# Turned rows in two tiles, and seven weight pieces split ahead of the last routing

## The chip, the core and the metric

The kernel runs on one core of a Trainium2 chip. What is measured is the device time of one execution, in microseconds (us), as the median of several runs. Engines are named as in the profile: PE is TensorE's matmuls and PEld its weight loads, DVE is VectorE, ACT is ScalarE, POOL is GpSimd, and SP is the engine that issues most DMAs. "SPq" marks what SP's sequencer does, the issuing of a DMA above all.

## The reference

Three layers run one after the other: an attention with capped scores, a dense gated MoE layer, and a sparse MoE with one expert for each token.

```python
# attention: B=4, H=12, S=448, D=64
scores = cap * tanh(q @ k.T / sqrt(D) / cap)
x = softmax(scores) @ v                       # then rows of 768 for 1792 tokens
# first MoE: 768 -> 1536 -> 768
x = (silu(x @ w_gate) * (x @ w_val)) @ w_out
# second MoE: 8 experts, 768 -> 1024 -> 768
do = x @ w_skip > 0                           # other tokens keep x
e = argmax(x[do] @ w_route); g = softmax(...)[e]
out[do] = x[do] + g * (relu(x[do] @ w1[e]) @ w2[e])
```

Products whose accuracy matters are made of three: each operand is split into a high and a low part (float32r), and high x high, high x low and low x high are added up in PSUM (`mm3`, `mm3_`).

## The kernel before

All instructions stand in an order that is written out by hand; on each engine they run in that order, and semaphores hold an instruction until what it reads is there.

The tokens come in four batch rows of 448. Attention works on pairs of heads, six pairs for a row. The first MoE of a row has 36 units: 24 of `g` and `v` (gate and value columns) and 12 of `y` (output columns, each in two halves). Unit `w` of 144 does 18 products of 128x448. `OPENING` is the order of the first row's attention; then `FIRST_UNITS` is the order inside each of the first 36 units and `UNITS` that of the others. While the units of row `b` run, the attention of row `b + 1` runs between them. In the first 36 units the weights also arrive as 64 bit numbers and are converted on DVE (`convert`), kept in DRAM (`keep_w`, tensor `ws`), and read again from there for the rows that follow (`load_w`, tile `raw64` of pool `r64`, four buffers). `round_w` (ACT) and `rest_w` (DVE) split a unit's weights two units ahead. "piece" in the unit orders is `load_w`, "loads" brings the heads of a later pair, "keep" is `keep_w`.

When an output column group is done (`rows_end`), `turn_rows` multiplies it with the routing weights on PE and turns it on DVE into the tile `row`, two units after; one unit later `store_rows` sends it to the output with four DMAs from SP ("store" in the orders). There is one buffer of `row`, and in the last batch row a second one, `so["row"]`, for odd groups. In `FIRST_UNITS` "store" is the last word, behind "piece", "keep" and "loads".

The second MoE works on slots: up to 128 tokens of one expert. An expert's weights come as eight pieces of 128x1536 (four of `w1`, four of `w2`). A piece is loaded by SP into a raw room (`so["raw"]`, `load_next`) and split into a pair of rooms (`so["pair"]`, `split_next`): ACT makes the high part, DVE the low part. `first(0)` to `first(3)` and `second(0)` to `second(3)` each use one piece; `piece()` hands it out, and once `so["auto"]` is set it splits ahead until `AHEAD` pieces are ready. Slot 0 holds tokens of the first three rows only. It is routed while the last row's units run; its expert's and slot 1's expert's weights are fetched early (`FETCHED`). `SPLITS` names the units, counted from the end, behind which one piece is split and another loaded. The last row's attention rooms serve as three raw rooms and three pairs (`open_early`), and two pairs more come from the first MoE's input (`more`).

After the last unit the left side's rooms are given back and `open_late` opens others: seven raw rooms, one pair, and tiles for the gathered rows. `LATE` is the order of what follows: the routing of the last row on DVE (`choose`, `ranks`, `gates`, `tiles`, `places`, `at`, `entries`, `listed`, `experts`) and, beside it, slot 0 on PE (`first1` to `second3`; `hidden0` and `hidden1` turn the hidden rows, `lows0` and `lows1` make their low parts; `split` splits one piece; `rows1` turns the input rows of slot 1). `gates` has an exponential on ACT, `count` two products on PE. When the list is there, POOL gathers the rows of slots 1 to 7 (`gather`). Slots 1 to 7 then run through `slot`.

At the very start `big` is loaded into a register of every engine: it chooses between two versions of the whole kernel, and the branch on it stands behind the first transposes.

Of the kernel before, what the change touches and what calls it, by code (L numbers as in the profile page):

```python
# [7 lines left out]
F32 = mybir.dt.float32  # L8
F32R = mybir.dt.float32r
# [17 lines left out]

LENGTHS = (5, 6, 5, 6, 5, 5)

AHEAD = 4  # L30

SPLITS = (11, 10, 9, 7, 6)


STEPS = {0: 6, 1: 2, 2: 3, 3: 3, 4: 3, 5: 4, None: 4}
# [16 lines left out]
""".split()  # L52
FIRST_UNITS = """
    out weigh sum scores1 roundw bits gate hidden after after after bits loww dn products both bits tanh1 exp1
    tanh2 exp2 turn abs bits split last bits scores2 bits piece keep loads logits count rows chain turnl store
""".split()
UNITS = """
    out turnl weigh sum scores1 scores2 products fold count logits rows hidden split loads tanh1 exp1 add1 turn
# [1 line left out]
    chain store  # L60
""".split()
LATE = """
    choose first1 count first2 hidden0 gates ranks tiles places lows0 at entries first3 split second0 listed hidden1
    gather experts lows1 second1 split second2 split rows1 second3 gather gather gather gather gather gather
""".split()


# [1 line left out]
def tile_attn_moe_moe(  # L69
# [15 lines left out]
    nc = tc.nc  # L85
    B, H, S, D = q.shape
# [9 lines left out]
    PIECE = 1536  # L96
# [12 lines left out]
    big_i = const.tile([128, 1], I32, name="big_i")  # L109
# [15 lines left out]
    count = const.tile([T, E], F32, name="count")  # L125
# [9 lines left out]
    rows = const.tile([T, 128], mybir.dt.bfloat16, name="rows")  # L135
# [245 lines left out]
    def whole(exact):  # L381
        with ExitStack() as ph:

            def pools(side):
                stack = ph.enter_context(ExitStack())

                def pool(name, bufs, **kw):
                    kw.setdefault("reuse_waits", "tile")
                    return stack.enter_context(tc.tile_pool(name=name, bufs=bufs, side=side, **kw))

                return stack, pool

            _, pool = pools("left")
            keep_p = pool("keep", 1)
            left, pool = pools("left")
            one_p = pool("one", 1)
            r64_p = pool("r64", 4)
            w_p = pool("w", 3)
            y_p = pool("y", 2)
            ps_v = pool("ps_v", 1, space=PSUM)  # L400
# [1 line left out]
            right, pool = pools("right")  # L402
# [208 lines left out]
            W_END = B * NU  # L611
# [72 lines left out]
            cur, terms = {}, {}  # L684
# [61 lines left out]
            def turn_rows(b, j):  # L746
                x2 = cur.pop(("x2", j))
                cur["lp", j] = lp = ps_m.tile([128, T], F32, name="mo")
                for c in range(NC):
                    nc.tensor.matmul(  # L750
                        lp[32 * c:32 * c + 32], lhsT=w9[:, j], rhs=x2[:, T * c:T * c + T], start=True, stop=True
                    )

                cur["row", j] = row = so["row"] if b == B - 1 and j % 2 else one_p.tile([128, S], F32, name="row")
                nc.vector.transpose(out=row, in_=x2)

            def store_rows(b, j):
# [58 lines left out]
            chain = [None, None]  # L816
# [13 lines left out]
            so = {"raw": [], "pair": [], "xg": [], "auto": False}  # L830
# [18 lines left out]
            def open_late():  # L849
                left.close()  # L850
                _, pool = pools("left")
                p = pool("late", 1)
                psum = pool("ps_l", 1, space=PSUM)
                so["xg"] += [p.tile([128, DM], F32, name=f"xg{i}") for i in range(1, NSTATIC)]
                so["raw"] += [p.tile([128, PIECE], F32, name=f"raw{i}") for i in range(7)]
                so["pair"] += [[p.tile([128, PIECE], F32R, name=f"{n}4") for n in ("gh", "gl")]]
                so["late"] = p.tile([T, 1600], F32, name="late_room")
                so["hid"] = p.tile([128, F2], F32, name="hid")
                so["o"] = [p.tile([128, DM], F32, name=f"o{i}") for i in range(3)]
                so["last"] = psum.tile([128, 512], F32, name="last")  # L860
                so["py"] = psum.tile([128, 2, 512], F32, name="py")
                for xg in so["xg"][1:]:
                    nc.gpsimd.memset(xg, 0.0)
# [27 lines left out]
            def turn_x(s):  # L891
                xh, xl = so["x"]
                for kk in range(0, KD, 3):
                    turned(xh[:, kk:kk + 3], xl[:, kk:kk + 3], so["xg"][s % NSTATIC][:, 128 * kk:128 * kk + 384])
# [100 lines left out]
            at = {load_part: 8}  # L995
# [158 lines left out]
            for w in range(W_END):  # L1154
                if w == W_END - NU:
                    open_early()
                unit(w)
                if w == W_END - NU + 2 * KF:

                    more = keep_p.tile([128, 2 * KD * S], F32R, tag="xhl", name="more")  # L1160
                    so["pair"] += [[more[:, 0:PIECE], more[:, PIECE:2 * PIECE]], [more[:, 2 * PIECE:3 * PIECE], so["odd"]]]
                    while load_next():
                        pass
                if w == W_END - 6:
                    while chain[0] is not None:
                        step("v", 1)
                        step("p", 1)
                    turn_x(0)
                if W_END - w in SPLITS:
                    split_next()  # L1170
                    load_next()
# [69 lines left out]
    with tc.manual_schedule():  # L1241
        nc.sync.dma_start(out=cap_sb, in_=cap.to_broadcast([128, 1]))
        for i, (queue, src) in enumerate(((nc.sync, q), (nc.scalar, k))):
            for j in range(2):
                queue.dma_start(out=first_pair()[:, i, :, j], in_=src[0, j].rearrange("(c p) d -> p c d", c=NC))
        for i in range(8):
            load_block(1, i)
        nc.gpsimd.memset(ident, 1.0)
        nc.gpsimd.affine_select(
            out=ident, in_=ident, pattern=[[1, 128]], compare_op=ALU.is_equal, fill=0.0, base=0,  # L1250
            channel_multiplier=-1,
        )
        nc.vector.memset(ones, 1.0)
        nc.scalar.activation(out=old, in_=ones[0:T, 0:1], func=ACTF.Tanh)
        nc.vector.tensor_reduce(
            alike[:, 0], ident.rearrange("p (a b) -> p b a", b=32), axis=AX.X, op=ALU.add
        )
        nc.vector.tensor_copy(alike[:, 1], alike[:, 0])
        nc.vector.memset(w9, 0.0)
        nc.vector.tensor_scalar(big_i, cap_sb, cap_sb, CAP_FAST * CAP_FAST, op0=ALU.mult, op1=ALU.is_gt)  # L1260
        nc.vector.tensor_scalar(inv_sb, cap_sb, float(D) ** 0.5, None, op0=ALU.mult)
        nc.vector.reciprocal(inv_sb, inv_sb)

        with tc.tile_pool(name="setup", bufs=5) as setup:

            def count_off(dst, **kw):
                ti = setup.tile(list(dst.shape), I32, name="ti")
                nc.gpsimd.iota(ti[:], **kw)
                nc.vector.tensor_copy(dst, ti)

            count_off(rank8, pattern=[[-1, E]], base=E, channel_multiplier=0)
            count_off(rows, pattern=[[1, 128]], base=1, channel_multiplier=0)
            count_off(steps, pattern=[[128, JM]], base=0, channel_multiplier=0)
            count_off(slots, pattern=[[1, MAXSLOT]], base=0, channel_multiplier=0)
            nc.vector.tensor_scalar(number, rank8, -1.0, float(E), op0=ALU.mult, op1=ALU.add)
            nc.vector.tensor_tensor(
                before, rank8.unsqueeze(1).to_broadcast([T, E, E]), rank8.unsqueeze(2).to_broadcast([T, E, E]),
                op=ALU.is_gt,
            )

            count_off(tok, pattern=[[T, NT]], base=-65536, channel_multiplier=1)
            nc.gpsimd.memset(oh, 0.0)
            nc.gpsimd.memset(above, 0.0)
            nc.gpsimd.affine_select(
                out=lt, in_=ones[0:T], pattern=[[1, T]], compare_op=ALU.is_ge, fill=0.0, base=0,
                channel_multiplier=-1,
            )

        with tc.tile_pool(name="first", bufs=2, space=PSUM) as first_p:
            for i in range(2):  # L1290
                ps = first_p.tile([128, S], F32, name="turned")
                for c in range(NC):
                    nc.tensor.transpose(
                        ps[:, T * c:T * c + T], first_pair()[:, i, c].rearrange("p h d -> p (h d)"), ident[0:T, 0:T]
                    )
                (nc.scalar.copy if i else nc.vector.tensor_copy)(first_turned()[:, i], ps)
        big = nc.values_load(big_i[0:1, 0:1], min_val=0, max_val=1)
        with tc.If(big > 0) as cmp:
            whole(True)
        with cmp.Else():  # L1300
            whole(False)
# [31 lines left out]
```

## Time and profile before

| | us |
|---|---|
| median of 3 runs | 926.13 |
| lowest and highest run | 925.58, 926.15 |
| the profiled execution | 925.63 |
| its span, first to last instruction | 923.8 |
| PE busy | 893.8 (97%) |
| DVE busy | 628.3 (68%) |
| ACT busy | 506.7 (55%) |
| POOL busy | 109.3 (12%) |

[...] Times in the rows below are microseconds from the start of the span. A row of the timeline gives the start, the duration (of all together where several instructions are merged), the engine, the line of the kernel, the operation with what it writes and reads, and in brackets how long the engine stood idle before it and what ended that. PE's matmuls overlap, so their durations are longer than the distance from one to the next.

### The profile page before, as it was taken

To read this page: it belongs to the slowest core of one execution; us is meant where nothing else is said; L and a number is where in the kernel's file an instruction comes from. 1 tells how busy PE (TensorE), PEld (TensorE's weight loads), DVE (VectorE), ACT (ScalarE), POOL (GpSimd) and SP (SyncE) were. 2 spreads that over 40 slices of the span, in tenths; PEclk is the share of its full clock that TensorE was granted. 3 is DMA by queue.
4 is the path that set the end of the run, shared out by engine and by line. 5 is a ranking of instruction groups with operands and counts; after the bars stand their busy time and mean duration, and the time that the engine had idled before them with its cause. 6 is when DMAs were issued, how large, how long until landed. Compare 5 with 4: busy or idle time off the path is not lost.

```text
span 923.8 us, 12689 instructions
## 1 busy us (share of the span) xinstructions
PE 893.8 (97%) x4700; PEld 696.2 (75%) x4700; DVE 628.3 (68%) x920; ACT 506.7 (55%) x587; POOL 109.3 (12%) x72
## 2 busy tenths in 40 slices
PE   5999999999799999999999999999999998899996
PEld 2336776677477877787778877889999887789996
DVE  2768999998637656654657656535765636999994
ACT  4995675657245455535546456223333423877782
POOL 1000000000002221222122230200000013110001
PEclk9999999999899999999999999999999998999999
DMA  6997889888676444524673322254262738999970
GB/s 120 185 241 205 229 235 252 235 243 230 161 151 166 107 97 100 132 53 96 142 168 113 85 78 91 66 133 147 69 240 73 236 72 313 360 381 348 382 251 7
DMA packets 226336, 161.50 MB, mean 175 GB/s; under 512 B 159180, under 2 KB 186828, under 8 KB 226256
## 3 DMA queue, kind: packets, MB, share of 16 engines
q1 hardware_dynamic: 224048, 157.12, 60.0%
q0 software_dynamic: 1280, 3.16, 1.0%
q8 instruction: 41, 0.67, 0.3%
q14 instruction: 39, 0.32, 0.1%
q10 hardware_dynamic: 928, 0.23, 0.1%
HBM read 140.80 MB, written 22.81 MB: 177 GB/s over the span
## 4 chain that ended last, share of the span: by engine, by line
PE 86%; DVE 5%; ACT 4%; DMA 2%; issue 2%; SPq 1%; POOL 0%; POOLq 0%; DVEq 0%; ACTq 0%
PE mo L680 19%; PE mo L682 17%; PE mo L681 17%; PE ps L458 7%; PE bank L513 6%; PE py L937 3%; PE py L936 3%; PE py L935 2%; PE ph L936 2%; PE ph L935 2%; PE ph L937 2%; PE tp L884 1%; PE mo L547 1%; ACT arena L467 1%; ACT arena L474 1%
## 5 line engine op out<-in xcount | busy, mean ns | idle before, releaser
L680 PE MATMUL mo<-xhl,wh 128*128 128x448 f32 x576 | 215.0, 373 | 0.0
L682 PE MATMUL mo<-xhl,wl 128*128 128x448 f32 x576 | 210.4, 365 | 0.0
L681 PE MATMUL mo<-xhl,wh 128*128 128x448 f32 x576 | 210.3, 365 | 0.0
L355 DVE TENSOR_TENSOR wl<-raw,wh 128x768 fp32r<-128x768 f32 x108 | 115.7, 1071 | 71.4 <-ACT wh L667 69.8
L667 ACT CAST wh<-raw 128x768 fp32r<-128x768 f32 x108 | 89.7, 831 | 87.9 <-PE mo L681 61.2
L680 PEld LDWEIGHTS mo<-xhl,wh 128*128 128x128 f32 x576 | 108.1, 188 | 27.3 <-issue 8.1
L682 PEld LDWEIGHTS mo<-xhl,wl 128*128 128x128 f32 x576 | 108.2, 188 | 8.9 <-DVE wl L355 0.2
L681 PEld LDWEIGHTS mo<-xhl,wh 128*128 128x128 f32 x576 | 108.3, 188 | 7.9
L680 PE MATMUL mo<-hh,wh 128*128 128x448 f32 x288 | 108.5, 377 | 0.3 <-ACT x L727 0.3
L682 PE MATMUL mo<-hh,wl 128*128 128x448 f32 x288 | 105.5, 366 | 0.0
L681 PE MATMUL mo<-hl,wh 128*128 128x448 f32 x288 | 105.5, 366 | 0.0
L719 ACT ACTIVATE s<-mo 128x448 f32<-128x448 f32 x48 | 26.0, 541 | 114.5 <-PE mo L682 111.6
L458 PE MATMUL ps<-qkt 64*112 64x448 f32 x368 | 82.6, 568 | 0.0
L467 ACT ACTIVATE arena<-ps,inv_sb 112x896 f32<-112x896 f32 x72 | 68.6, 1004 | 5.6 <-PE ps L458 5.5
L502 POOL TENSOR_TENSOR sums<-arena 112x896 f32<-112x896 f32 x11 | 23.3, 2114 | 394.5 <-ACT arena L474 394.5
L474 ACT ACTIVATE arena<-arena,cap_sb 112x1792 f32<-112x1792 f32 x36 | 64.5, 1792 | 1.1
L680 PEld LDWEIGHTS mo<-hh,wh 128*128 128x128 f32 x288 | 54.3, 189 | 13.3 <-issue 8.7
L722 DVE SCALAR_TENSOR_TENSOR s<-s,mo 128x448 f32<-128x448 f32 x48 | 29.6, 617 | 42.6 <-PE mo L682 42.3
L682 PEld LDWEIGHTS mo<-hh,wl 128*128 128x128 f32 x288 | 54.2, 188 | 4.6
L681 PEld LDWEIGHTS mo<-hl,wh 128*128 128x128 f32 x288 | 54.4, 189 | 4.1
L513 PE MATMUL bank<-arena,arena 112*64 112x448 f32 x264 | 54.9, 548 | 1.6 <-ACT w L638 0.8
L458 PEld LDWEIGHTS ps<-qkt 64*112 64x112 f32 x368 | 29.6, 175 | 34.9 <-issue 29.3
(257 smaller groups left out, 1430.1 us busy)
## 6 DMA issues: line engine op xcount, KB each, us to landing
raw<-ws SPq DMA_DIRECT2D x54, 768.0 KB, 4.8
raw<-in_moe_w_dram SPq DMA_DIRECT2D x41, 768.0 KB, 6.6
ws<-w SPq DMA_DIRECT2D x36, 384.0 KB, 5.9
pair_room<-in_moe_w_dram SPq DMA_DIRECT2D x16, 768.0 KB, 6.6
raw<-in_moe_w_gate_dram SPq DMA_DIRECT2D x12, 768.0 KB, 5.3
raw<-in_moe_w_val_dram SPq DMA_DIRECT2D x12, 768.0 KB, 5.8
raw<-in_moe_w_out_dram SPq DMA_DIRECT2D x12, 768.0 KB, 5.2
arena<-in_v_dram SPq DMA_DIRECT2D x24, 224.0 KB, 5.1
```

The source lines that it names most:

```text
L355: engine.tensor_tensor(low, full, high.bitcast(F32), op=ALU.subtract)
L458: nc.tensor.matmul(ps[:, i, 0:S], lhsT=qkt[rows_, 1, T * c:T * c + T], rhs=qkt[rows_, 0], start=True, stop=True)
L467: nc.scalar.activation(out=t[:, j], in_=ps[:, :, 0:S], func=ACTF.Tanh, scale=inv_sb[0:T])
L474: nc.scalar.activation(out=ts[part], in_=ts[part], func=ACTF.Exp, scale=cap_sb[0:T])
L513: nc.tensor.matmul(pv[64 * i:64 * i + 64], lhsT=hd["vn"][:, i, c], rhs=hd["t"][c // 2][:, c % 2, i], start=c == 0, stop=c == NC - 1,)
L667: nc.scalar.copy(wh, w32s[w])
L680: nc.tensor.matmul(ps, lhsT=wh, rhs=mh, start=start, stop=False)
L681: nc.tensor.matmul(ps, lhsT=wh, rhs=ml, start=False, stop=False)
L682: nc.tensor.matmul(ps, lhsT=wl, rhs=mh, start=False, stop=stop)
L935: nc.tensor.matmul(ps, lhsT=sh, rhs=wh, start=start, stop=False)
L936: nc.tensor.matmul(ps, lhsT=sh, rhs=wl, start=False, stop=False)
L937: nc.tensor.matmul(ps, lhsT=sl, rhs=wh, start=False, stop=stop)
```

## The change

- `FIRST_UNITS`: "store" moves from the end of a unit to a place ahead of "piece".
- `row` gets two buffers.
- Pool `r64` moves to the part of the left side that stays open to the end, so its four rooms outlive the first MoE. Ahead of the splits behind the last two units, two pairs are made of these four rooms. `SPLITS` gets the entries 2 and 1: two more pieces are split behind units 142 and 143, and two more loaded.
- `open_late` opens five raw rooms instead of seven and no pair. So there are eight raw rooms in all instead of ten, and seven pairs instead of six.
- `AHEAD` is 5 instead of 4.
- `LATE`: "ranks" and then "gates" come right behind "count", before "first2" and "hidden0" (before: "gates" then "ranks" behind "hidden0"). The last "split" stands behind "rows1" instead of ahead of it.
- The register load of `big` stands ahead of the first transposes.

```diff
-AHEAD = 4
-
-SPLITS = (11, 10, 9, 7, 6)
+AHEAD = 5
+
+LATER = 5
+SPLITS = (11, 10, 9, 7, 6, 2, 1)
 FIRST_UNITS = """
     out weigh sum scores1 roundw bits gate hidden after after after bits loww dn products both bits tanh1 exp1
-    tanh2 exp2 turn abs bits split last bits scores2 bits piece keep loads logits count rows chain turnl store
+    tanh2 exp2 turn abs bits split last bits scores2 bits store piece keep loads logits count rows chain turnl
 LATE = """
-    choose first1 count first2 hidden0 gates ranks tiles places lows0 at entries first3 split second0 listed hidden1
-    gather experts lows1 second1 split second2 split rows1 second3 gather gather gather gather gather gather
+    choose first1 count ranks gates first2 hidden0 tiles places lows0 at entries first3 split second0 listed hidden1
+    gather experts lows1 second1 split second2 rows1 split second3 gather gather gather gather gather gather
             keep_p = pool("keep", 1)
+            r64_p = pool("r64", 4)
             left, pool = pools("left")
             one_p = pool("one", 1)
-            r64_p = pool("r64", 4)
-                cur["row", j] = row = so["row"] if b == B - 1 and j % 2 else one_p.tile([128, S], F32, name="row")
+                cur["row", j] = row = so["row"] if b == B - 1 and j % 2 else one_p.tile([128, S], F32, name="row", bufs=2)
-                so["raw"] += [p.tile([128, PIECE], F32, name=f"raw{i}") for i in range(7)]
-                so["pair"] += [[p.tile([128, PIECE], F32R, name=f"{n}4") for n in ("gh", "gl")]]
+                so["raw"] += [p.tile([128, PIECE], F32, name=f"raw{i}") for i in range(LATER)]
+                if W_END - w in (1, 2):
+
+                    so["pair"] += [[r64_p.tile([128, PIECE], F32R, tag="raw64", name=n) for n in ("gh", "gl")]]
                 if W_END - w in SPLITS:
                     split_next()
                     load_next()
+        big = nc.values_load(big_i[0:1, 0:1], min_val=0, max_val=1)
         with tc.tile_pool(name="first", bufs=2, space=PSUM) as first_p:
...
-        big = nc.values_load(big_i[0:1, 0:1], min_val=0, max_val=1)
         with tc.If(big > 0) as cmp:
```

## Rows read from the trace of the kernel before

**Rows 1.** The page: busy time of PE, and one group of DMA issues.

```profile
PE 893.8 (97%) x4700; PEld 696.2 (75%) x4700; DVE 628.3 (68%) x920; ACT 506.7 (55%) x587; POOL 109.3 (12%) x72
...
raw<-in_moe_w_dram SPq DMA_DIRECT2D x41, 768.0 KB, 6.6
```

**Rows 2.** The timeline of DVE where the first row's units turn output rows.

```profile
228.76 0.27 DVE L768 COPY lgt<-mo 128x112 f32<-128x112 f32 x1
239.24 0.65 DVE L755 STREAM_TRANSPOSE row<-x 128x448 f32<-128x448 f32 x1 [10.21 <-DMA out_dram<-row]
...
245.68 0.64 DVE L572 STREAM_TRANSPOSE dn<-mo 128x448 f32<-128x448 f32 x1
```

**Rows 3.** The timeline of SP in the same stretch.

```profile
228.91 0.39 SPq L619 DMA_DIRECT2D raw<-ws  x1
...
232.76 4.77 SPq L761 DMA_DIRECT2D out_dram<-row  x4
```

**Rows 4.** The timeline of PE in the same stretch.

```profile
236.25 0.94 PE L547 MATMUL mo<-head_room,ones 112*32 112x448 f32 x8
...
246.38 0.39 PE L578 MATMUL bank<-dn,alike 64*64 64x14 f32 x4 [5.28 <-DVE dn L572]
```

**Rows 5.** Stretches of 1 us: length, busy us by engine, granted clock, DMA share, GB/s.

```profile
245.00:246.00 1.00, 0.00 (x0) 0.00 (x0) 1.00 (x2) 1.00 (x2) 0.00 (x0) 0.61 1.01 267
252.00:253.00 1.00, 1.00 (x6) 0.92 (x6) 0.96 (x2) 0.00 (x0) 0.00 (x0) 0.98 1.02 409
...
774.00:775.00 1.00, 1.00 (x6) 1.00 (x5) 0.97 (x4) 0.00 (x0) 0.00 (x0) 0.64 1.01 393
...
781.00:782.00 1.00, 1.00 (x5) 0.70 (x5) 1.00 (x2) 0.11 (x1) 1.00 (x1) 0.95 0.53 128
```

**Rows 6.** The timeline of DVE in the last routing and slot 1.

```profile
768.39 0.19 DVE L212 TENSOR_REDUCE gate<-late_room 112x4 f32<-112x32 f32 x1 [3.71 <-ACT late_room L211]
...
772.12 0.68 DVE L355 TENSOR_TENSOR rl<-tp,rh 128x512 fp32r<-128x512 f32 x1
...
774.49 1.75 DVE L355 TENSOR_TENSOR gl<-head_room,gh 128x1536 fp32r<-128x1536 f32 x1
776.89 0.20 DVE L1191 TENSOR_TENSOR lists<-lists,last 128x42 f32<-128x42 f32 x1 [0.64 <-PE last L256]
...
778.92 0.67 DVE L355 TENSOR_TENSOR rl<-tp,rh 128x512 fp32r<-128x512 f32 x1
...
784.66 1.02 DVE L355 TENSOR_TENSOR xgl<-tp,xgh 128x384 fp32r<-128x384 f32 x2 [1.46 <-ACT xgh L885]
786.59 1.02 DVE L969 SCALAR_TENSOR_TENSOR o<-py,lists,xg 128x768 f32<-128x768 f32 x1 [0.91 <-PE py L937]
...
797.53 0.69 DVE L355 TENSOR_TENSOR rl<-tp,rh 128x512 fp32r<-128x512 f32 x1
```

**Rows 7.** The timeline of PE in the last routing and slot 1.

```profile
764.63 0.39 PE L195 MATMUL last<-above,ones 112*112 112x40 f32 x2 [0.18 <-DVE above L188]
...
772.86 0.44 PE L937 MATMUL py<-more,rl 128*128 128x384 f32 x1 [2.82 <-DVE rl L355]
...
783.62 0.60 PE L884 MATMUL tp<-ident,xg 128*128 128x128 f32 x4
...
789.33 0.50 PE L936 MATMUL ph<-gl,xgh 128*128 128x512 f32 x1 [2.40 <-DVE gl L355]
...
797.95 0.34 PE L935 MATMUL py<-gh,rh 128*128 128x384 f32 x1
```

**Rows 8.** POOL's first gather in the timeline, and the landing of all eight gathers.

```profile
778.10 1.01 POOL L870 DMA_INDIRECT xg<-out_dram,idx  x1 [14.64 <-DVE late_room L231]
...
DMA to landing us min/median/max: 3.8/6.7/8.0
```

**Rows 9.** The timeline of DVE behind the last unit's products.

```profile
758.96 0.27 DVE L770 TENSOR_TENSOR lgt<-lgt,mo 128x112 f32<-128x112 f32 x1 [6.97 <-PE mo L750]
```

**Rows 10.** The timeline of ACT in the opening.

```profile
19.49 0.92 ACT L638 ACTIVATE w<-raw 128x768 f32<-128x768 f32 x1 [0.34 <-DMA raw<-in_moe_w_gate_dram]
```

## The prediction

> **What bounds the kernel now.** I read the page first: TensorE (PE) is busy for 97% of the span [rows 1], so a change pays only where PE waits or runs at its lower clock, or if it gives PE less to do. This change leaves PE's work as it is. So I went through the busy time of 10 to 100 us stretches and looked for those in which PE is not full. Four are left: the opening, a hole near 245 us, two holes between 770 and 790 us, and the end after the last product. Everywhere else PE is at 100%, so what a stage saves stays saved: behind each hole PE alone sets the pace.
>
> The hole near 245 us: PE waits 5.28 us for a transposition on VectorE (DVE) [rows 4]. DVE is late because it stood idle for 10.21 us before it could write the second turned row [rows 2]: the single row tile was still being stored. SP issued that store at 232.76 us, although DVE had turned the row before it went on to the work at 228.76 us: SP first stood before a piece load that it got out at 228.91 us, and then issued keeps and loads [rows 3]. The granted clock shows what follows: it falls at about 245.4 us and is back at 252 us [rows 5].
>
> The holes of the last routing: PE waits 2.82 us for the low half of the turned hidden rows, then 2.40 us for the first split of slot 1 [rows 7]. After the first the clock is at its lower level from about 774.3 to 781.1 us [rows 5]; after the second it doesn't fall.
>
> **The change part by part.**
>
> **Two row tiles, and the store ahead of the piece load.** The second row goes to its own tile, so DVE's idle 10.21 us ends [rows 2] (two later and far shorter waits of this kind lie beside full PE and are worth nothing). Next late: the transposition that PE waited for needs the sum products, which start at 236.25 us and take 0.94 us [rows 4]; DVE does it by 237.8 us, and PE wants it at 246.38 - 5.28 = 241.1 us. So the wait goes whole, with 3.3 us to spare. The clock's fall goes with it: from 246.38 to 252.0 us PE worked 5.6 us at half its speed, of which half, 2.8 us, comes back; I take 2.6, since not every instruction there doubled. Sum: 5.3 + 2.6 = **7.9 us**. On SP the four stores now stand in front of the piece load, the keep and the pair loads. If they take as long as before, 4.77 us [rows 3], the piece load moves from 228.91 to at most 232 us; it is fetched five units ahead, some 20 us before its use, so this costs nothing. What else is queued behind it, a pair load, is used at the end of the pair's next round, also over 8 us later. If that cover were gone, it would cost 3 us.
>
> **Two more splits before the routing.** Each is a copy on ScalarE (ACT) and a subtraction on DVE, 1.75 us as at 774.49 [rows 6]. They are placed where DVE stands idle for 6.97 us [rows 9] and ACT at least as long, and two splits need 3.5 us: nothing is pushed. Their rooms are those of the first MoE's weights, whose last reader on DVE has ended by then. DVE now turns one row after the first split instead of before it, and SP stores it some 3 us later, but still ahead of the last row's store. Cost 0; without the cover 3.5 us.
>
> **Gates after the ranks, their exponential issued first.** DVE waits 3.71 us for that exponential [rows 6], since ACT had the turned hidden rows ahead of it. Now ranks can begin when the count is there, at 764.63 + 0.39 us [rows 7], and the exponential is done meanwhile. The whole DVE chain moves up by 3.3 us. The low half (772.12 to 772.80 us) is ready at 769.5 us, before PE asks for it at 772.86 - 2.82 = 770.04 us. So the 2.82 us and the lower clock behind it go: from 772.86 us to the next wait at 786.93 us PE needed 14.1 us, 6.7 of them at half speed, so 10.7 us at full speed.
>
> **What is late next.** DVE reaches split 8 at 768.8 + (774.49 - 772.12) = 771.2 us, waits about 0.3 for ACT's copy, splits for 1.75, and has the list at 773.4: 3.45 earlier than at 776.89 [rows 6]. Tables and the second half's low part took 778.92 + 0.67 - 776.89 = 2.7 more: 776.1 us. PE asks for it earlier: from 770.04 us come the rest of second 0 (1.7), the list's products and the second turn (0.8 and 0.4, half of what they took at the lower level), second 1 (2.1) and two products of second 2 (0.35): 775.4. A new wait of 0.7 us; then PE is done with second 2 at 777.9. The gather of slot 1 goes out 3.45 us earlier, at 774.65 us [rows 8]. Nothing shows when the first one landed, but the shortest took 3.8 us [rows 8], and this one was in use at 783.62 [rows 7], so 3.8 to 5.5 us. I take the shorter, since two fewer loads run beside it: 778.45 us, and PE waits 0.6 (to 2.2) us. So slot 1 begins at 770.04 + 10.7 + 0.7 + 0.6 = 782.0 us, and the 2.40 us wait is gone because two pieces lie ready there. From that point to the second half's first product PE took 797.95 - 789.33 = 8.6 us [rows 7], and 0.35 later it asks for the low part of the hidden rows: at 791.0 us.
>
> Is DVE there? In the kernel before, from the first low part (772.12) to this one (797.53) DVE took 25.4 us [rows 6]. One split of (797.53 - 786.59 - 1.02) / 6 = 1.65 us drops out: eight fall there instead of nine, since AHEAD rises by one as two are done early. Its idle times there, 0.64 + 1.46 + 0.91 us, drop out as well. New ones come in: 0.3 for ACT's copy of split 8; 2.0 until the rows of slot 1 are gathered and turned; 0.95 for ACT's copy of split 10, now behind the turned rows. So it starts at 768.8 + 25.4 - 1.7 - 3.0 + 3.3 = 792.8 us and ends at 793.4. PE waits 2.4 us there, and goes on at 793.4 where it was at 798.3: **4.9 us** gained. If the gather takes 5.5 us it is 3.2; if DVE held nothing up there, 7.3.
>
> [...]
>
> **Fewer raw rooms, AHEAD 5.** Eight instead of ten rooms, seven pairs instead of six. PE takes a piece in 8.62 / 4 = 2.15 us at least [rows 7], so a room comes round in 8 x 2.15 = 17.2 us, of which 1.75 are the split and some 0.4 SP's: a load may take 15 us, and the median is 6.6 [rows 1]. Cost 0.
>
> **The branch's register load ahead of the first transposes.** PE's idle time before its first scores gets shorter by an unknown part. But ACT, which feeds on them, waits at 19.49 us for a weight transfer [rows 10] that SP issues behind its own branch, and SP has nothing between the load's old and new place. PE and ACT then only wait longer. I take 0; bounds are 0.3 us each way, about ACT's wait there.
>
> **Sum:** 7.9 + 4.9 = 12.8 us. The profiled execution took 925.63 us (923.8 of span and 1.8 around it); its successor should take 912.8. The median of the runs, 926.13, lies 0.5 above it: **913.3 us**.
>
> **The rivals.** *The clock falls once more.* The new waits of 0.7, 0.6 to 2.2 and 2.4 us lie within 18 us. For it: a wait of 2.82 us was followed by 6.7 us at the lower level [rows 5, 7]. Against it: one of 2.40 us was not. It would cost another 3.3 us: 916.6 us. [...] *The gather of slot 1 lands late*, 5.5 us after its issue instead of 3.8: it is the end that the rows allow, and it makes DVE's chain 1.7 us longer: 915.0 us. For it: gathers there took up to 8.0 us [rows 8]. Against it: the first finds fewer loads and no other gather ahead of it. [...] *The row wait moves instead of going*: the stores sit in SP's one queue and wait for a DVE that is one unit behind, so the piece load or the third row comes late in turn. For it: SP already stood 3 us before that load. Against it: 3.3 us of slack, and 8 or more on the loads. Then only the tail pays: 926.1 - 4.9 = 921.2 us. *Slower:* eight rooms starve slots 2 to 7. Each microsecond of landing time above 15 costs 1/8 per piece, 6 us over 48 pieces; it eats the whole gain from 15 + 12.8/6 = 17.1 us on, and at 18 us the time is 913.3 + 18 = 931 us. For it: through slots 1 to 6 these loads follow each other without a pause. Against it: their median of 6.6 us.
>
> **How the numbers follow.** Forecast 0.50, late gather 0.12, clock 0.18, row wait 0.10, starving 0.05, something that cancels out 0.05 (0.03 of it within 0.2%, the rest still faster). A measurement of this kernel can tell about 0.2%, 1.9 us, from no change. So faster 0.92, same 0.03, slower 0.05. The range goes down to 926.1 - 7.9 - 7.3 - 0.3 = 910.6 (DVE holds nothing up) and up to the clock case with the slow gather, 916.6 + 1.7 = 918.3, say 918.5; outside are the row and starving cases.
>
> **What would show it.** Right: no DVE wait for the row store and no PE gap near 241 us, with the clock at its upper level through 240 to 255 us; no wait of PE for the first low part; a PE wait of some 2 us for the low part in slot 1, and PE there 4 to 5 us earlier than the first gain alone gives. Wrong: a PE gap that stays near 245 us; the lower level between 775 and 800 us; PE waits for loads or splits in slots 2 to 7; a shift of more than 0.3 us at 30 us.

## The result and the profile after

The changed kernel takes **913.86 us** (median of 4 runs, 913.43 to 914.47) where the kernel before took 925.86 us beside it: a ratio of 0.9871, with a 95% interval of 0.9854 to 0.9888. The forecast was 913.3 us. The total came out within 0.6 us, but two of its terms did not: the opening, put at nothing, brought about 1.5 us, and the tail, put at 4.9 us, brought 1.9 in the profiled execution.

To see that, cut the span at two products of PE that stand in both kernels: the one that starts the unit ahead of the first turned rows, and the first one behind the last routing weights. They are the first and second line of PE's timeline here, of the kernel before:

```profile
226.79 0.47 PE L680 MATMUL mo<-hh,wh 128*128 128x448 f32 x1 [0.29 <-ACT x L727]
...
761.91 0.32 PE L775 MATMUL mo<-ident,lgt 128*112 128x128 f32 x1 [0.40 <-DVE lgt L770]
```

and of the changed kernel:

```profile
225.24 0.47 PE L681 MATMUL mo<-hh,wh 128*128 128x448 f32 x1 [0.42 <-ACT x L728]
...
752.17 0.32 PE L776 MATMUL mo<-ident,lgt 128*112 128x128 f32 x1 [0.40 <-DVE lgt L771]
```

| us of the span | before | after | gained | forecast |
|---|---|---|---|---|
| opening, to the first mark | 226.8 | 225.2 | 1.5 | 0 |
| middle, between the marks | 535.1 | 526.9 | 8.2 | 7.9 |
| tail, from the second mark | 161.9 | 160.0 | 1.9 | 4.9 |
| span | 923.8 | 912.2 | 11.6 | 12.8 |

**Middle.** DVE's timeline of the changed kernel, where [rows 2] showed an idle time of 10.21 us, then SP's and PE's of the same stretch:

```profile
226.97 0.64 DVE L756 STREAM_TRANSPOSE row<-x 128x448 f32<-128x448 f32 x1
...
235.72 0.65 DVE L573 STREAM_TRANSPOSE dn<-mo 128x448 f32<-128x448 f32 x1 [2.24 <-PE mo L548]
```

```profile
225.21 3.71 SPq L762 DMA_DIRECT2D out_dram<-row  x4
229.03 0.41 SPq L620 DMA_DIRECT2D raw<-ws  x1
```

```profile
239.49 0.29 PE L579 MATMUL bank<-dn,alike 64*64 64x14 f32 x4
```

No row waits for a store any more. The transposition `dn` is ready 3 us before PE wants it, and the 5.28 us of [rows 4] are gone. The granted clock stays at its upper level through the whole stretch, where [rows 5] had it fall (length, busy us of each engine, granted clock, DMA share, GB/s):

```profile
240.00:245.00 5.00, 5.00 (x30) 3.68 (x25) 4.93 (x8) 1.43 (x3) 0.00 (x0) 1.00 0.94 267
245.00:250.00 5.00, 5.00 (x32) 4.22 (x31) 2.64 (x5) 4.49 (x5) 0.00 (x0) 1.00 0.89 190
```

**Tail.** PE's timeline of the changed kernel: the 2.82 us of [rows 7] are gone, and these three waits stand there instead.

```profile
766.42 0.44 PE L937 MATMUL py<-gh,rl 128*128 128x384 f32 x1 [0.62 <-DVE es_i L325]
...
770.27 0.87 PE L884 MATMUL tp<-ident,xg 128*128 128x128 f32 x6 [1.82 <-DMA xg<-out_dram,idx]
...
784.85 0.62 PE L937 MATMUL py<-gh,rl 128*128 128x384 f32 x1 [2.30 <-DVE rl L356]
```

The gather for the second of them, on POOL, and the DVE rows around it:

```profile
764.87 1.02 POOL L870 DMA_INDIRECT xg<-out_dram,idx  x1 [11.15 <-DVE late_room L232]
```

```profile
766.30 1.74 DVE L356 TENSOR_TENSOR gl<-head_room,gh 128x1536 fp32r<-128x1536 f32 x1
771.37 1.02 DVE L356 TENSOR_TENSOR xgl<-tp,xgh 128x384 fp32r<-128x384 f32 x2 [3.33 <-ACT xgh L885]
```

And the granted clock behind the third wait, columns as above:

```profile
784.00:785.00 1.00, 0.15 (x1) 0.15 (x2) 1.00 (x3) 0.19 (x1) 0.00 (x0) 0.97 0.99 406
785.00:786.00 1.00, 1.00 (x4) 1.00 (x5) 1.00 (x1) 0.00 (x0) 0.00 (x0) 0.50 1.02 405
...
788.00:789.00 1.00, 1.00 (x8) 0.90 (x7) 0.13 (x1) 0.11 (x1) 0.00 (x0) 0.82 1.04 418
```

So the forecast had the waits of 0.7 and 2.4 us right (0.62 and 2.30). The gather's wait is 1.82 us, not 0.6; and the clock fell, which cost 1.7 us (the sum of what the 1-us stretches lack to 1.00). 4.9 - 1.2 - 1.7 = 2.0 us, against 1.9 measured. These are two of the prediction's rivals, the late gather and the clock, and both came about in this execution.

### The profile page after: what moved, and what is told of

The parts are those of the page before. It is cut to its first block, busy times and chain, and to the rows that moved or that the text cites. A ratio compares the mean times of both kernels' runs of the same rounds, so it can differ in the third digit from the quotient of the medians.

```text
span 912.2 us, 12700 instructions
## 1 busy us (share of the span) xinstructions
PE 888.3 (97%) x4700; PEld 693.0 (76%) x4700; DVE 627.7 (69%) x920; ACT 506.7 (56%) x587; POOL 108.8 (12%) x72
## 4 chain that ended last, share of the span: by engine, by line
PE 86%; ACT 5%; DVE 4%; DMA 2%; issue 2%; SPq 0%; POOL 0%; POOLq 0%; DVEq 0%; ACTq 0%
PE mo L681 19%; PE mo L683 18%; PE mo L682 18%; PE ps L459 7%; PE bank L514 6%; PE py L937 2%; PE py L935 2%; PE py L936 2%; PE ph L935 2%; PE ph L937 2%; PE ph L936 2%; PE mo L548 2%; ACT arena L468 1%; PE tp L884 1%; ACT arena L475 1%
```

## The experiments

Each was timed beside runs of the kernel before, whose medians there were 925.48, 924.86 and 925.84 us. The first table gives the medians, the second the cut of the profiled execution at the two marks, PE's waits in the tail, and what the lower clock cost in the tail ahead of the last products (again what the stretches lack to 1.00; in e12 and e10 PE stood idle in part of that time, so there it cost less).

| run | median us | lowest, highest | ratio, 95% interval |
|---|---|---|---|
| e1_load_back | 914.61 | 913.43, 916.42 | 0.9889, 0.9872 to 0.9906 |
| e2_two_tiles | 918.59 | 917.94, 920.91 | 0.9928, 0.9914 to 0.9941 |
| e3_store_first | 919.51 | 918.09, 919.62 | 0.9931, 0.9917 to 0.9944 |
| e4_tail_only | 921.36 | 920.45, 921.98 | 0.9955, 0.9942 to 0.9969 |
| e5_ahead4 | 912.16 | 910.14, 913.68 | 0.9861, 0.9842 to 0.9880 |
| e6_gates_back | 917.88 | 913.20, 920.03 | 0.9924, 0.9906 to 0.9941 |
| e7_split_back | 910.88 | 910.55, 913.66 | 0.9854, 0.9836 to 0.9872 |
| e8_list_first | 911.36 | 910.93, 912.12 | 0.9850, 0.9834 to 0.9866 |
| e9_all_three | 908.34 | 907.27, 909.69 | 0.9808, 0.9794 to 0.9822 |
| e11_list_ahead4 | 909.17 | 908.45, 909.96 | 0.9821, 0.9809 to 0.9834 |
| e12_no_early_splits | 921.51 | 920.11, 922.89 | 0.9955, 0.9942 to 0.9968 |
| e10_loads_after_gather | 918.90 | one run | |

| trace | opening | middle | tail | PE's waits in the tail | clock |
|---|---|---|---|---|---|
| before | 226.8 | 535.1 | 161.9 | 2.82, 2.40 | 3.4 |
| after | 225.2 | 526.9 | 160.0 | 0.62, 1.82, 2.30 | 1.7 |
| e1 | 227.6 | 526.9 | 157.6 | 0.63, 1.38, 2.29 | 0 |
| e2 | 228.5 | 526.9 | 163.8 | 2.81, 0.43, 2.40 | 5.1 |
| e3 | 227.9 | 527.6 | 162.2 | 2.81, 2.40 | 3.4 |
| e4 | 225.8 | 534.6 | 159.5 | 0.62, 1.55, 2.30 | 1.7 |
| e5 | 226.7 | 527.0 | 156.3 | 0.62, 1.61, 0.63 | 0 |
| e6 | 225.1 | 526.9 | 159.5 | 2.81, 0.29, 0.36, 2.28 | 0 |
| e7 | 225.2 | 526.9 | 156.8 | 0.62, 1.79, 0.99 | 0 |
| e8 | 226.8 | 526.9 | 156.0 | 0.18, 2.28 | 0 |
| e9 | 226.5 | 526.9 | 153.8 | 0.97 | 0 |
| e11 | 225.6 | 526.9 | 154.2 | 0.28, 0.62 | 0 |
| e12 | 225.3 | 526.9 | 166.2 | 0.29, 1.90, 1.99, 1.22, 2.35 | 6.8 |
| e10 | 225.7 | 526.9 | 164.6 | 0.62, 1.92, 1.30, 4.20 | 3.4 |

The middle repeats to 0.1 us where nothing in it differs, and the tail follows its waits and the clock. The opening varies by 1.7 to 2.7 us between executions of the same order, so a difference of medians below 2 us is read with the table, not alone.

### Is the opening the register load?

The changed kernel with that line back in its old place:

```diff
-        big = nc.values_load(big_i[0:1, 0:1], min_val=0, max_val=1)
         with tc.tile_pool(name="first", bufs=2, space=PSUM) as first_p:
...
+        big = nc.values_load(big_i[0:1, 0:1], min_val=0, max_val=1)
         with tc.If(big > 0) as cmp:
```

> The changed kernel with the register load back behind the first transposes. Theory (the move is worth what the two traces differ by in the opening, 1.5 to 1.6 us, where the prediction said 0): 913.9 + 1.6 = 915.4 us, the first ACT abs again near 19.5 us with a wait for DMA, everything after it about 1.5 us later than in the changed kernel, and no other difference. Rival (the opening differs from one execution to the next, and the move is worth nothing): 913.9 us, within 0.5 us, and the abs falls where it likes.

914.61 us, halfway between the two, with an interval that holds both. In the trace the abs starts at 18.66 us with no wait for DMA, not near 19.5, so this part of the expectation failed. The traces tell more, because every other run also has the load in one place or the other. SP's first transfer behind the branch, before and after:

```profile
11.72 0.32 SPq L440 DMA_DIRECT2D arena<-in_v_dram  x1
```

```profile
11.16 0.32 SPq L441 DMA_DIRECT2D arena<-in_v_dram  x1
```

In the five traces with the old place (before, e1 to e4) it starts at 11.56 to 11.89 us, in the nine others at 11.03 to 11.28. PE's first scores start at 10.54 to 11.16 us, against 10.14 to 10.56. So what stands behind the branch on these two engines starts 0.5 us earlier in the mean, and that is the load's work. From there to the first mark the difference of the means grows to 1.5 us (227.3 against 225.8), but the two groups overlap there (225.8 to 228.5, and 225.1 to 226.8): what is over 0.5 us hangs on when the second weight lands, for which ACT waited 0.37 to 2.63 us, and isn't settled.

### Which half of the row edit?

Two tiles alone, on the kernel before:

```diff
-                cur["row", j] = row = so["row"] if b == B - 1 and j % 2 else one_p.tile([128, S], F32, name="row")
+                cur["row", j] = row = so["row"] if b == B - 1 and j % 2 else one_p.tile([128, S], F32, name="row", bufs=2)
```

> The kernel before with the second tile for the turned rows alone; the store stays behind the piece. Theory (the tile is what DVE waited for, and who issues the store first no longer matters once there are two): the waits of DVE for the stores are gone, 925.9 - 7.9 = 918.0 us. Rival (the store's place among SP's transfers counts too, because the piece that waits ahead of it holds it up): part of the gain only, 920 to 923 us, with DVE still waiting for a row's store.

The store ahead of the piece alone, also on the kernel before:

```diff
-    tanh2 exp2 turn abs bits split last bits scores2 bits piece keep loads logits count rows chain turnl store
+    tanh2 exp2 turn abs bits split last bits scores2 bits store piece keep loads logits count rows chain turnl
```

> The kernel before with the store ahead of the piece alone; one tile for the turned rows. Theory (it was the piece's wait on SP that held the store up, so with the store first the second row waits only about 2 to 3 us for a store of that length, which is less than the slack in front of the next PE matmul that needs it): nearly all of the 7.9 us as well, 918 to 920 us. Rival (one tile is what counts, DVE's wait stays long): 923 to 926 us.

Either edit gives it. Two tiles alone bring the middle to 526.9 us, the value of the whole change: all 8.2 us. The median shows 6.9 of them. The profiled execution is the slowest of the five: its opening is 1.7 us and its tail 1.9 us longer than before. The store alone brings 527.6 us, 7.5 of the 8.2. Here are DVE and PE of the second kernel:

```profile
235.30 0.65 DVE L755 STREAM_TRANSPOSE row<-x 128x448 f32<-128x448 f32 x1 [5.14 <-DMA out_dram<-row]
241.74 0.64 DVE L572 STREAM_TRANSPOSE dn<-mo 128x448 f32<-128x448 f32 x1
```

```profile
242.44 0.29 PE L578 MATMUL bank<-dn,alike 64*64 64x14 f32 x4 [0.20 <-DVE dn L572]
```

DVE still waits 5.14 us for the store (more than the 2 to 3 us expected), but the slack ahead of PE takes nearly all of it: 0.20 us are left. The forecast's view that the wait goes, and that its length beyond the slack was the cost, holds; that both edits are needed was never claimed, and they aren't.

### The tail without the rest

The changed kernel with one tile, the old order of units and the old load:

```diff
-    tanh2 exp2 turn abs bits split last bits scores2 bits store piece keep loads logits count rows chain turnl
+    tanh2 exp2 turn abs bits split last bits scores2 bits piece keep loads logits count rows chain turnl store
...
-                cur["row", j] = row = so["row"] if b == B - 1 and j % 2 else one_p.tile([128, S], F32, name="row", bufs=2)
+                cur["row", j] = row = so["row"] if b == B - 1 and j % 2 else one_p.tile([128, S], F32, name="row")
...
-        big = nc.values_load(big_i[0:1, 0:1], min_val=0, max_val=1)
...
+        big = nc.values_load(big_i[0:1, 0:1], min_val=0, max_val=1)
```

> The changed kernel without the register load's move, the second tile and the store's move: only the seven pieces, the rooms and the gates' order are left. By the two traces the tail brings 2.2 us: 925.9 - 2.2 = 923.7 us, with PE's wait for the gathered rows, its wait for the low part of slot 1 and the lower clock after it. By the prediction's term it brings 4.9 us: 921.0 us. Rival (the clock's fall in the tail needs the earlier start that the rows give, and is absent here): 922.0 us.

921.36 us is close to the forecast's 921.0, but for a wrong reason: of the 4.0 us between the two profiled spans (923.8 and 919.8) 1.0 stands in the opening and 0.6 in the middle. The tail has the waits and the lower clock of the changed kernel, and brings 2.4 us.

### What held the low part of slot 1 up?

One split fewer ahead:

```diff
-AHEAD = 5
+AHEAD = 4
```

> The changed kernel with AHEAD 4 in place of 5: one split fewer stands on DVE ahead of slot 1's low part. Theory (the wait of 2.30 us for that low part is DVE's queue, and the lower clock after it comes of that wait): the low part is out about 1.7 us earlier, PE's wait falls to about 0.6 us, the clock stays up: 913.9 - 1.7 - 1.6 = 910.6 us. Rival (DVE only fills the time with a wait for the next piece, the split comes back later on the path): 913.9 us. Between them: the wait goes, the clock falls anyway, 912.2 us.

The last split in its old place:

```diff
-    gather experts lows1 second1 split second2 rows1 split second3 gather gather gather gather gather gather
+    gather experts lows1 second1 split second2 split rows1 second3 gather gather gather gather gather gather
```

> The changed kernel with the last split ahead of the row's second part again, as before the change. Theory (DVE stands idle for 3.33 us for the gathered rows' high part, the split fits there and leaves the place ahead of slot 1's low part, which comes 1.7 us earlier): PE's wait of 2.30 us falls to about 0.6 us and the clock stays up, 913.9 - 3.3 = 910.6 us. Rival (the split is not done by the time that the gathered rows come, and holds up the row's second part as much as it gains): 913.9 us, or up to 1.7 us more.

Both do it. PE's rows for that low part, first with AHEAD 4, then with the split moved:

```profile
784.47 0.45 PE L937 MATMUL py<-gh,rl 128*128 128x384 f32 x1 [0.63 <-DVE rl L356]
```

```profile
783.25 0.45 PE L937 MATMUL py<-gh,rl 128*128 128x384 f32 x1 [0.99 <-DVE rl L356]
```

2.30 us become 0.63 and 0.99, one split of 1.75 us on DVE less in the way, and the clock stays up. The tails are 156.3 and 156.8 us, 3.7 and 3.2 below the changed kernel's. So DVE's queue of splits set that wait, as the forecast said. With the split moved, DVE does it in the 3.33 us in which it stood idle for the gathered rows. So AHEAD 5 and the last split's new place, two parts of the change, made it slower: the wait is 1.7 and 1.3 us longer with them, and without them the medians are 912.16 and 910.88 us. That the clock stays up can't be put down to the edits alone: in e1, which has the changed kernel's tail, it stayed up behind 2.29 us.

### The gates, and the two early splits

The gates back behind the first piece's first half:

```diff
-    choose first1 count ranks gates first2 hidden0 tiles places lows0 at entries first3 split second0 listed hidden1
+    choose first1 count first2 hidden0 gates ranks tiles places lows0 at entries first3 split second0 listed hidden1
```

> The changed kernel with the gates and ranks in their old place, behind the first piece's first half. Theory (the list, and with it the gather, comes later by the work that is put ahead of the ranks, up to 3.3 us, and PE's wait of 2.82 us in the opening of the tail returns): 913.9 + 3 = 917 us, up to 919 if the clock falls once more. Rival (the gather's landing rules and the splits that were moved ahead of the routing made the gain): 914 to 915 us.

And five pieces split ahead of the last routing, not seven:

```diff
-SPLITS = (11, 10, 9, 7, 6, 2, 1)
+SPLITS = (11, 10, 9, 7, 6)
```

> The changed kernel with five pieces split ahead of the last routing, as before, in place of seven; the gates' new place, the rooms and the rest stay. Theory (the two splits of 1.7 us each now stand on DVE's path in slot 1): the low part of slot 1 comes 3.4 us later, PE's waits there grow from 2.30 to some 5.7 us, and the clock falls in more of the executions: 913.9 + 3.4 = 917.3 us, up to 920. Rival (the gates' place made the gain of the tail alone): 914 us.

With the gates back the wait returns:

```profile
763.03 0.44 PE L937 MATMUL py<-more,rl 128*128 128x384 f32 x1 [2.81 <-DVE rl L356]
```

The median is 917.88 us, as expected. The profiled execution is the fastest of six (913.20 us, mean granted clock 0.998): the clock did not fall there behind the 2.81 us. The five others have 0.990 to 0.994 and 915.96 to 920.03 us, so there the clock seems to have fallen. In the trace the other waits are shorter with the gates back (0.29 for 0.62, 0.36 for 1.82), so the waits add up to 5.7 us against 4.7: of the 2.81 us that the gates' new place takes off the first wait 1.8 come back, most of it at the gather, and 1.0 is left. The rest of the 4.0 us between the medians would be the clock and the opening.

Without the early splits it is 921.51 us, above the range expected: the tail is 166.2 us, 4.3 longer than in the kernel before. I had looked for the price in slot 1. Most of it comes earlier: PE waits 1.90, 1.99 and 1.22 us for pieces while slot 0 is still running, then 2.35 for the first one of slot 1, and the clock is down for much of 773 to 787 us. Two tiles alone, with the old tail, took 918.59 us. Neither tail edit without the other (917.88 and 921.51 us, both with the register load moved, the new rooms and AHEAD 5) is clearly better than that, and both together are (913.86). So the two edits need each other; that the gates bring the routing forward on a DVE that must then have less left to split is the reading of these waits, not shown by itself.

### Why the gather came late

Hold the five late loads on SP until the gathered rows are there:

```diff
+                if so.get("wait"):
+                    return False
...
+                    if so.pop("wait", False):
+                        nc.sync.dma_start(out=probe, in_=so["xg"][s][0:1, 0:16])
+                        while load_next():
+                            pass
...
-            so["auto"] = False
-            while load_next():
-                pass
+            so["wait"] = True
```

> A measurement, not a better version: the changed kernel with its five late loads held back on SP until the rows of slot 1 have been gathered (SP first stores a few of the gathered numbers to a scratch place, which waits for the gather). Theory (the gather waits for the loads that are still moving when it is issued; in the changed kernel they move at a share of 0.99 to 1.04 until 768 us, 3 us behind its issue): with none moving, PE's first transposition of the gathered rows comes at most 4 us after the issue instead of 5.4, and its wait of 1.82 us shrinks to 0.4 us or less; later PE waits for the pieces that came late. Rival (the gather takes 5 us whatever else moves): 5.0 to 5.4 us again.

And a version that only issues fewer loads ahead of the gather: the third split of the tail, which frees a room and so lets SP issue one load, moves behind the list.

```diff
-    choose first1 count ranks gates first2 hidden0 tiles places lows0 at entries first3 split second0 listed hidden1
-    gather experts lows1 second1 split second2 rows1 split second3 gather gather gather gather gather gather
+    choose first1 count ranks gates first2 hidden0 tiles places lows0 at entries first3 second0 listed hidden1
+    gather experts lows1 second1 split split second2 rows1 split second3 gather gather gather gather gather gather
```

> The changed kernel with the third split of the tail moved from ahead of the second half's first part to behind its second part. Theory (the second half's first part and the list are no longer held up by that split, the PE's wait of 0.62 us goes and the gather is issued about 0.9 us earlier): about 0.9 us less, 913.0 us. Rival (the gather lands no earlier for an earlier issue, or the low part of slot 1 comes later by the split that now stands closer to it): 913.9 to 915 us.

The two stretches of 1 us from 766 us on, first in the changed kernel, then with the list first, then with the loads held:

```profile
766.00:767.00 1.00, 0.57 (x3) 0.58 (x4) 1.00 (x2) 0.00 (x0) 0.81 (x1) 1.00 1.02 375
767.00:768.00 1.00, 1.00 (x8) 1.00 (x7) 1.00 (x1) 0.00 (x0) 0.70 (x2) 1.00 0.99 351
```

```profile
766.00:767.00 1.00, 1.00 (x7) 1.00 (x6) 0.97 (x6) 1.00 (x2) 0.71 (x1) 1.00 1.03 406
767.00:768.00 1.00, 1.00 (x7) 0.80 (x6) 1.00 (x2) 1.00 (x1) 0.99 (x1) 1.00 0.41 139
```

```profile
766.00:767.00 1.00, 0.38 (x3) 0.10 (x1) 0.96 (x4) 0.00 (x0) 0.69 (x2) 1.00 0.01 0
767.00:768.00 1.00, 1.00 (x6) 1.00 (x7) 1.00 (x1) 0.00 (x0) 0.70 (x2) 1.00 0.10 19
```

The last two columns are the DMA share and GB/s. In the changed kernel the loads move at full rate until nearly 768 us, some 3 us behind the issue at 764.87, and PE's first transposition of the gathered rows follows the issue by 5.40 us. With the list first (issue at 765.70) they are through soon after 767 us, some 1.5 us behind it, and PE follows in 3.77 us. With the loads held PE waits for the gather no more; the small store that waits for the gathered rows is through on SP 3.2 us behind the issue:

```profile
765.35 1.01 POOL L871 DMA_INDIRECT xg<-out_dram,idx  x1 [11.16 <-DVE late_room L233]
```

```profile
768.26 0.29 SPq L1214 DMA_DIRECT2D probe<-xg  x1
```

In e6 the gather is issued later, at 767.52 us, and the queues are nearly empty at that moment; only the load that SP got out at 766.44 us is still to move:

```profile
766.00:767.00 1.00, 1.00 (x9) 1.00 (x7) 0.93 (x5) 0.62 (x2) 0.00 (x0) 1.00 0.11 32
767.00:768.00 1.00, 1.00 (x8) 1.00 (x7) 0.93 (x6) 1.00 (x1) 0.48 (x1) 1.00 0.32 77
...
769.00:770.00 1.00, 0.92 (x5) 0.92 (x6) 1.00 (x2) 0.00 (x0) 0.84 (x1) 1.00 1.01 403
770.00:771.00 1.00, 1.00 (x7) 0.79 (x5) 0.69 (x1) 0.00 (x0) 0.85 (x1) 1.00 0.48 96
```

It moves until 770 us, and PE follows the gather's issue in 3.95 us. In e9 (below), issued at 765.31 with the loads moving to 767.6, PE follows in 4.54, and in e1, e4, e5 and e7, which keep the changed kernel's order up to the gather, in 4.97 to 5.37. So PE gets the gathered rows some 2 us (1.5 to 2.5) after the loads that SP issued ahead of the gather have drained. That later pieces came late when the loads were held (waits of 1.92, 1.30 and 4.20 us) is why it isn't a version to keep. e8 is: its tail is 156.0 us, 4.0 less than the changed kernel's. The waits that went (0.62, and 1.64 of 1.82) and the clock that stayed up (1.7) make just that. Only the waits are the edit's: the wait of 2.28 us for the low part is still there, and in e1 the clock stayed up behind such a wait without this edit.

### Put together

The list first and AHEAD 4 (e11); and both with the last split ahead of the turned rows as well (e9, whose edit is shown):

```diff
-AHEAD = 5
+AHEAD = 4
...
-    choose first1 count ranks gates first2 hidden0 tiles places lows0 at entries first3 split second0 listed hidden1
-    gather experts lows1 second1 split second2 rows1 split second3 gather gather gather gather gather gather
+    choose first1 count ranks gates first2 hidden0 tiles places lows0 at entries first3 second0 listed hidden1
+    gather experts lows1 second1 split split second2 split rows1 second3 gather gather gather gather gather gather
```

> The changed kernel with the third split of the tail behind the second half's second part, and AHEAD 4. Theory (the two edits act on different waits, the first on those of 0.62 and 1.82 us, the second on that of 2.30 us, and without them the clock stays up): from the last routing to the end PE takes 148.54 - 1.67 = 146.9 us instead of 152.49, so 913.9 - 5.6 = 908.3 us. Rival (one split fewer early is missing later): 910 to 911 us, with new waits of PE for splits in slots 2 to 7.

> The changed kernel with all three edits of the runs before: AHEAD 4, the third split behind the second half's second part, and the last split ahead of the row's second part. In the trace of the run with the list first, the part from the last routing to the end took 148.54 us of PE, with one wait of 2.28 us left, for the low part of slot 1; DVE was never idle there for the gathered rows. Theory (DVE is full, so a split put ahead of the gathered rows only changes places: it gives back at the rows what it takes at the low part): no better than the list first with AHEAD 4 alone, 908.2 to 909.5 us. Rival (each edit pays what it paid alone): 907.8 us or less.

909.17 and 908.34 us: both beat the changed kernel by some 5 us, and the kernel before by 1.8 and 1.9%. Their tails are 154.2 and 153.8 us. In the first the waits are where the sum put them (0.28 and 0.62 us). In the second the 0.62 at the low part is gone, and PE waits longer for the gather itself:

```profile
769.85 0.88 PE L884 MATMUL tp<-ident,xg 128*128 128x128 f32 x6 [0.97 <-DMA xg<-out_dram,idx]
```

That wait can't be put down to the split: the two orders are the same up to the gather, but in this execution SP got its five loads out at 2.3 us behind the second mark, where in e11 it was 1.7. 0.8 us between the medians can't be told from nothing here. That fits the expectation of a DVE that is full, and doesn't show it.

## Why the prediction was right or wrong

- **Turned rows, 7.9 us: right**, 8.2 measured. The wait went whole and the clock's fall with it (by its row the clock fell at 245.2 us, not 245.4; nothing hangs on that); SP's stores took 3.71 us, and no load behind them came late. The rival that the wait moves did not show.
- **Early splits hidden: right.** DVE does them from 742.99 and 745.22 us on, and is idle for 2.29 us before the next product it has to add up arrives at 749.23 us.
- **Gates, and the first low part: right.** The 2.82 us are gone, and come back with the gates (2.81). Net of the longer waits that follow, 1.0 us of PE's waiting is left, as e6 shows.
- **The new waits of 0.7 and 2.4 us: right**, 0.62 and 2.30.
- **The gather, 0.6 us: wrong**, 1.82. The term took the shortest landing, 3.8 us, on the argument that two fewer loads run beside it. But the last of those that do run (SP at 763.78 us, 1.1 ahead of the gather) was freed by the split ahead of "second0", which stands there before the change too; with that split behind the list (e8) the wait is 0.18. The kernel before shows such loads as well: the DMA share was 1.05 and 1.02 from 778 to 780 us, behind its gather's issue at 778.10. So the rival of the late gather came, with its 5.5 us nearly to the digit (5.40), and DVE's idle time for the rows, put at 2.0 us, was 3.33. POOL's own instruction doesn't tell an early landing from a late one: for this gather it took 1.01 or 1.02 us in each of the 13 traces in which it was read (all but e3).
- **The clock: wrong in the profiled execution.** The forecast counted on the 2.40 us wait that had not lowered it. The wait of 2.30 us did; it cost 1.7 us, where the rival was priced at 3.3. The four executions have mean granted clocks of 0.996, 0.996, 0.996 and 0.998 (0.991 in the profiled execution of the kernel before), so it seems to have stayed up in one. That the lower level is about half speed, which the terms of 2.6, 10.7 and 3.3 us take for granted, was measured: the granted clock is 0.50 of the upper one in each us from 246 to 252 and from 775 to 781 in the kernel before, and products of 128x448 start 0.37 or 0.38 us apart there at 251 us, against 0.20 or 0.21 in the changed kernel at 250 us.
- **Eight rooms cost nothing: right.** No wait of PE for a load in slots 2 to 7.
- **The register load, 0 us: wrong**, at least 0.5, and the prediction's own sign of it came: by ACT's split of the second weight (26.72 us before, 25.05 after) the shift was 1.7 us. The argument was that SP issues the weights behind its own branch and isn't moved. SP's first transfer behind the branch is moved by 0.5 us, though its own register load stands at 7.2 us in the changed kernel and at 7.3 before.
- **The sum** came out by compensation: +1.5 in the opening and +0.3 in the middle, -1.2 for the gather and -1.7 for the clock make 11.7, against 11.6 measured and 12.8 forecast.

## What to carry to other kernels

When a list is made earlier so that a gather can start earlier, look at what the transfer queues hold at that moment: loads that were issued ahead of it landed first here (they moved until nearly 768 us, and PE had the rows at 770.27), and moving the split that frees a room behind the gather took 2.3 us off PE's waits, where the gates' new place had taken 1.0. On an engine that makes pieces ahead, the number made ahead is a delay for everything queued behind them: one fewer took 1.7 us off a wait here. Cut the span at products that stand in both kernels before you credit a total to an edit: here wrong terms of either sign gave a right sum.

## What the hardware did that was not expected

- **The same wait lowers the clock or doesn't.** Waits of 2.28 to 2.40 us for PE in the tail were followed by the lower level (a granted clock of 0.50) in three traces (the changed kernel, e2, e4) and not in five (before, e1, e3, e6, e8). Waits of 2.81 or 2.82 us were, in three of four. A fall cost 1.7 us in the first case, 3.4 in the second. In e12 the clock fell behind a wait of 1.99 us already (one of 1.90 had ended 5 us before), and its wait of 2.35 us lies in the stretch at the lower level. What decides between the two is not shown. So a forecast that hangs on one such wait should carry both ends.
- **Behind the branch an engine stands for some 3 us.** In the changed kernel SP's branch stands at 8.1 us and its first transfer at 11.16, before at 8.2 and 11.72; PE's row for the branch takes 3.79 us, before 3.99. What holds the engines there is not shown. Between 6 and 12 us the queue that the page calls q14, instruction, moves 4 packets in the kernel before and in e1, which have the load's old place, and 7 in the changed kernel; no run shows whether that has to do with it. Why SP's restart moved by 0.5 us while its branch moved by 0.1 stays open; the engine whose branch stands last is ACT before (8.5 us) and SP after.
